# A retention, routed-experts and MLP kernel in which the conversion of the float64 weights, the experts' low parts and the second expert product are rewritten

## The chip, the cores and the metric

One core of a Trainium2 chip runs the whole program. The metric is the device time of one execution in microseconds (us), as the median of several runs. Times inside the execution come from one profiled execution of the kernel before.

Engines are named as the profile names them: PE is TensorE (PEld its weight loads), DVE is VectorE, ACT is ScalarE, POOL is GpSimd, SP is SyncE, which here only issues DMAs.

## What is computed

The reference has three parts, one behind the other, on 4608 tokens of 512 features:

```python
# retention: 8 batches x 8 heads, 576 positions, 64 features a head
scores = (1 / sqrt(64)) * q @ k.T
Dmat = where(rel >= 0, gamma[h] ** rel, 0)             # rel = i - j
x = (scores * Dmat) @ v                                # -> [4608, 512]

# routed experts: the tokens with a positive skip score, each to one of 8
do_compute = x @ w_skip > 0
xc = x[do_compute]
logits = xc @ w_gate
e_idx = argmax(logits, axis=1); gate = softmax(logits)[e_idx]
y = gate * (maximum(xc @ w1[e_idx], 0) @ w2[e_idx])    # w1 512x1024, w2 1024x512
x[do_compute] = xc + y

# MLP: w_in 512x2048 and w_out 2048x512 are float64
h = x @ w_in
out = (h * clip(h + 3, 0, 6) / 6) @ w_out
```

All inputs but `w_in` and `w_out` are float32. Those two arrive as float64 bits, and the kernel makes float32 pairs of them itself.

## The kernel before

**Numbers as pairs.** Products of float32 numbers are taken in the matmul type float32r. A factor is split into a high part (the number rounded to float32r) and a low part (the number less its high part), and a product is three matmuls: high by high, low by high, high by low. So every weight and every activation needs a copy (the high part, mostly on ScalarE) and a subtraction (the low part, on VectorE or GpSimd).

**Stages.** `phase_a` is the retention and the routing: a loop over 35 token tiles of 128 (`scale`, `scores`, `state`, `decay`, `rows`, the gate's products, and, four tiles at a time, the routing), then the last tile's routing, and eight blocks of the MLP's first product for 256 early tokens. `phase_b` is the experts, with more of the early blocks beside and behind the last one. `phase_c` is the MLP: 9 groups of 512 tokens by 16 blocks of inner features.

**Experts.** An expert takes 336 tokens, three tiles of 112 (`CT`). Its weights are 8 chunks of 128x1024 float32. The loop is over 8 experts `e` and 8 steps `f`, one step for 128 of the 1024 inner features. In a step, `mm1(e, f)` is 12 matmuls of 336 columns (line 889) into `h`; ScalarE makes `hh` (line 892), VectorE `hl` (line 894). Two steps later `mm2` is 12 matmuls of 336 columns (line 905): the weights are the stationary operand, and the four results `y` hold features on partitions and tokens in columns. Behind the last step of an expert, `y_out` copies the four `y` to `ys` in SBUF (lines 914 and 916), and `finish` turns them back to token rows with four transposes a tile (line 923), scales by the gate and adds the old row (line 925, VectorE), and scatters the rows to the table `xd` with an indirect DMA on GpSimd's queue (line 927). `finish` of expert e-1 stands in steps 2, 3 and 4 of expert e. `gather(e + 2)` stands in step 6 (line 865, three indirect DMAs); the rows of expert e+1 are turned in steps 5, 6 and 7: four transposes, then ScalarE's high part (line 881) and VectorE's low part (line 882) of `x`.

**The experts' weights.** A chunk is loaded into one of three buffers `raw` by SP, its high part is made by ScalarE (`chunk_hi`, line 156), its low part by GpSimd (`chunk_lo`, line 159). `pump_load`, `pump_hi` and `pump_lo` run ahead of the use, the low part 6 chunks (`LEAD`), the load 9. All 64 chunks pass in this way, six of them during the tile loop.

**The float64 weights.** They are taken in pieces of 256 columns (`CW`): 16 in the tile loop (`PARTX`, for the early blocks), 36 in the experts (`PART1`, stored as pairs to `wsc` in DRAM and loaded again later), 12 in the MLP (`PART2`). For a piece, `conv1` is six VectorE instructions on the two 32-bit words of each number (lines 207 to 217): four that build float32 bits from the high word `b`, two that turn the low word into a correction `a`. `conv_hi` is ScalarE's high part of `b`. `conv2` is two VectorE instructions: `b` less its high part (line 237), and `a` added to that (line 238). Three pieces are in work at a time, one stage apart.

**What sets the order.** Each engine runs its instructions in the order of the program text (`manual_schedule`), so the place of a call in a loop is its place in the engine's queue. A pool's buffer is handed to the next user when all readers of the last one are through.

Of the kernel before, what the change touches and what calls it, by code (L numbers as in the profile page):

```python
# [8 lines left out]
F32 = mybir.dt.float32  # L9
# [24 lines left out]
CONV_F = (0, 1, 3, 5, 6, 7)  # L34
# [21 lines left out]
def retention_moe_mlp_kernel(  # L56
    ctx: ExitStack,
    tc: tile.TileContext,
    qkv: bass.AP,      # [NT, 128, 4, 512]: q^T, k^T, k, v of a tile
    wg: bass.AP,       # [512, 32]: 8 gate columns, the skip column, zeros  # L60
# [8 lines left out]
    w_in, w_out = w_in.bitcast(I32), w_out.bitcast(I32)     # float64, as pairs of words  # L69
# [4 lines left out]
    ide = small[:, 0:4].rearrange("p (t c) -> p t c", c=2)        # early tokens  # L74
    ido = small[:, 4:10].rearrange("p (t c) -> p t c", c=2)       # the others of their tiles
# [4 lines left out]
    chp = prep.enter_context(tc.tile_pool(name="chp", bufs=3, side="right"))  # L80
    xp = prep.enter_context(tc.tile_pool(name="xp", bufs=1, side="right"))
# [35 lines left out]
    # ---------------------------------------------------------------- weights  # L117
    # chunk: [128, 1024] of float32 as two float32r parts, high and low
# [16 lines left out]
    # a chunk's place: the expert's 16 in turn, then the first the places that come free first  # L135
# [22 lines left out]
    def chunk_lo(i):  # L158
        nc.gpsimd.tensor_tensor(out=w_t[i][:, 1, :], in0=raw_t.pop(i), in1=w_t[i][:, 0, :].bitcast(F32), op=ALU.subtract)  # L159
# [24 lines left out]
    AH = [((f // 8) * 4, f % 8 // 2) for f in A_F[::2]]      # chunk of the first features, piece: a column group of xw  # L184
    PX = [(c + k, h) for c, h in AH for k in range(KD)]
# [4 lines left out]
    xw = {}            # w_in for the blocks A_F by feature tile; what they make behind it  # L190

    def conv_load(j):
        c, h = PIECES[j]
        src = chunk_src(64 + c)
        if c >= 8:
            src, h = src[:, h // (CN // 2), :], h % (CN // 2)
        r = cvp.tile([P, CW, 2], I32, tag="raw64", name="raw64")
        nc.sync.dma_start(out=r.rearrange("p n c -> p (n c)"), in_=src[:, h * 2 * CW:(h + 1) * 2 * CW])
        raw64[j] = r

    def conv1(j):
# [1055 lines left out]
```

## Time and profile before

| | us |
|---|---|
| median of 3 runs | 1425.91 |
| lowest, highest | 1423.62, 1426.36 |
| span of the profiled execution | 1422.7 |
| TensorE busy in it | 1293.4 (91%) |
| VectorE busy | 695.7 (49%) |
| ScalarE busy | 401.7 (28%) |
| GpSimd busy | 518.3 (36%) |

For the profiled execution the profile gives the span, from the first instruction to the last, and no time beside it; the median of the runs is 3.2 us above that span.

How the views are read. A stretch of the profiled execution is given as start:end in us from its start. The view by stretch shows its length and then, for PE, PEld, DVE, ACT and POOL, the busy time with the number of instructions, and last the granted clock of TensorE (1.00 is full speed), the mean busy share of the 16 DMA engines, and GB/s. The view by line gives the line of the code, the engine, the operation, output<-inputs by their names in the program, the tile's shape and type, the number of instructions, busy us, the mean ns of one, and the idle time of the engine before them with what ended it. In the view of waits, "PE h L889 <- DVE x L882" means that TensorE's instructions at line 889 waited for VectorE's at line 882. Busy time includes what an instruction spends waiting once it has begun.

### The profile page before, as it was taken

How to read it: one execution, taken by the hardware profiler on the slowest of the kernel's cores; microseconds unless marked ns; L12 is line 12 of the kernel's file. 1: busy time of each engine (PE TensorE's matmuls, PEld its weight loads, DVE VectorE, ACT ScalarE, POOL GpSimd, SP SyncE). 2: the span in 40 equal slices, each digit the busy share in tenths (PEclk: the TensorE clock that was granted, in tenths of full speed). 3: DMA queues.
4: the chain of work that ended last, by engine and by line, in shares of the span. 5: the costliest groups of instructions: out<-in, count | busy, mean ns of one | idle time of the engine just before them, and what ended most of it. 6: DMA issues, size and time to landing. Idle time of an engine off the chain costs nothing.

```text
span 1422.7 us, 20460 instructions
## 1 busy us (share of the span) xinstructions
PE 1293.4 (91%) x7973; PEld 1103.3 (78%) x7973; DVE 695.7 (49%) x1277; ACT 401.7 (28%) x724; POOL 518.3 (36%) x396
## 2 busy tenths in 40 slices
PE   8886878987788678999999999999999999999995
PEld 6665656986788677988888888888888888888884
DVE  6999998699999998259111111111111111111110
ACT  2222222533333333233222222222222222222221
POOL 4556455745664555222223222223222222222221
PEclk9999899998898888999999999999999999999998
DMA  9989683646565665853101000001000010000000
GB/s 349 255 244 304 219 294 127 202 154 197 181 199 175 195 205 168 333 200 104 67 1 42 26 23 30 23 8 37 23 30 17 14 38 23 30 1 1 30 0 31
DMA packets 71492, 163.60 MB, mean 115 GB/s; under 512 B 10420, under 2 KB 26804, under 8 KB 65504
## 3 DMA queue, kind: packets, MB, share of 16 engines
q1 hardware_dynamic: 63840, 146.38, 31.2%
q0 software_dynamic: 6592, 15.01, 3.4%
q8 instruction: 64, 1.05, 0.3%
q10 hardware_dynamic: 960, 0.86, 0.2%
q14 instruction: 36, 0.29, 0.1%
HBM read 121.47 MB, written 41.52 MB: 115 GB/s over the span
## 4 chain that ended last, share of the span: by engine, by line
PE 69%; DVE 25%; issue 2%; DMA 2%; ACT 0%; POOL 0%; SPq 0%; ACTq 0%; DVEq 0%; POOLq 0%
PE o L1102 28%; PE ch L1077 26%; DVE cvb L237 6%; PE y L905 4%; PE h L889 4%; DVE cva L207 3%; DVE ret L407 2%; DVE cva L209 2%; PE eh L269 2%; DVE kp L387 1%; DVE st L441 1%; DVE cvb L213 1%; PE cpt L1066 1%; DVE hl L894 1%; PE xTp L463 1%
## 5 line engine op out<-in xcount | busy, mean ns | idle before, releaser
L1077 PE MATMUL ch<-cx,w 128*128 128x512 f32 (+1 forms) x1728 | 397.6, 379 | 0.0
L1088 POOL TENSOR_TENSOR gl<-gt,gh 128x512 fp32r<-128x512 f32 (+1 forms) x144 | 178.2, 1237 | 601.2 <-ACT gh L1087 597.7
L1081 DVE SCALAR_TENSOR_TENSOR gt<-r,ch 128x512 f32<-128x512 f32 (+1 forms) x144 | 94.7, 658 | 579.3 <-ACT r L1079 579.3
L1102 PE MATMUL o<-w,gh 128*128 128x512 f32 x1120 | 377.8, 398 | 0.0
L1077 PEld LDWEIGHTS ch<-cx,w 128*128 128x128 f32 x1728 | 313.3, 188 | 66.1
L1102 PEld LDWEIGHTS o<-w,gh 128*128 128x128 f32 x1120 | 210.7, 188 | 47.9
L1102 PE MATMUL o<-w,gl 128*128 128x512 f32 x560 | 221.5, 395 | 0.0
L1079 ACT ACTIVATE r<-ch,small 128x512 f32<-128x512 f32 (+1 forms) x144 | 95.5, 663 | 431.4 <-PE ch L1077 431.4
L889 PE MATMUL h<-x,w 128*128 128x336 f32 x768 | 139.3, 332 | 63.9 <-DVE x L882 39.5
L889 PEld LDWEIGHTS h<-x,w 128*128 128x128 f32 x768 | 127.6, 200 | 67.9 <-DVE x L882 41.7
L159 POOL TENSOR_TENSOR w<-raw,w 128x1024 fp32r<-128x1024 f32 x64 | 152.4, 2397 | 60.5 <-ACT w L156 60.1
L905 PE MATMUL y<-hh,w 128*128 128x336 f32 x512 | 138.3, 337 | 0.0
L1087 ACT CAST gh<-gt 128x512 fp32r<-128x512 f32 (+1 forms) x144 | 86.1, 598 | 137.3 <-DVE gt L1081 136.8
L1102 PEld LDWEIGHTS o<-w,gl 128*128 128x128 f32 x560 | 105.5, 188 | 22.9
L237 DVE TENSOR_TENSOR cvb<-cvb,cvh 128x256 f32<-128x256 f32 x36 | 100.3, 2786 | 0.0
L905 PEld LDWEIGHTS y<-hh,w 128*128 128x128 f32 x512 | 95.9, 201 | 0.0
L905 PE MATMUL y<-hl,w 128*128 128x336 f32 x256 | 84.3, 329 | 0.0
L156 ACT CAST w<-raw 128x1024 fp32r<-128x1024 f32 x64 | 67.1, 1050 | 55.3 <-DMA raw<-in_w_dram 54.2
L467 ACT COPY xT<-xTp 128x512 f32<-128x512 f32 x36 | 21.1, 585 | 157.4 <-PE xTp L463 157.4
L892 ACT ACTIVATE hh<-h 128x336 fp32r<-128x336 f32 x64 | 28.8, 450 | 107.7 <-PE h L889 107.4
L927 POOL DMA_INDIRECT xd<-xr,ent x24 | 23.0, 957 | 88.1 <-DVE xr L925 86.4
L429 POOL TENSOR_TENSOR old<-st,cst 128x512 f32<-128x512 f32 x24 | 35.1, 1463 | 50.5 <-DVE st L441 33.8
(177 smaller groups left out, 1387.4 us busy)
## 6 DMA issues: line engine op xcount, KB each, us to landing
in<-in_qkv_dram SPq DMA_DIRECT2D x33, 1024.0 KB, 7.2
raw<-in_w_dram SPq DMA_DIRECT2D x64, 512.0 KB, 4.9
w<-wsc SPq DMA_DIRECT2D x13, 1024.0 KB, 9.6
xd<-row SPq DMA_DIRECT2D x36, 256.0 KB, 8.1
wsc<-cvh SPq DMA_DIRECT2D x36, 256.0 KB, 4.1
raw<-in_w_in_dram SPq DMA_DIRECT2D x32, 256.0 KB, 6.5
raw<-in_w_out_dram SPq DMA_DIRECT2D x32, 256.0 KB, 2.8
cr<-xd SPq DMA_DIRECT2D x31, 256.0 KB, 2.7
```

What stands on the lines that cost most here:

```text
L156: nc.scalar.copy(out=w_tile(i)[:, 0, :], in_=raw_t[i])
L159: nc.gpsimd.tensor_tensor(out=w_t[i][:, 1, :], in0=raw_t.pop(i), in1=w_t[i][:, 0, :].bitcast(F32), op=ALU.subtract)
L207: nc.vector.tensor_scalar(out=a, in0=hi32, scalar1=0x07FFFFFF, scalar2=3, op0=ALU.bitwise_and, op1=ALU.logical_shift_left)
L237: nc.vector.tensor_tensor(out=b.bitcast(F32), in0=b.bitcast(F32), in1=hl[:, 0, :].bitcast(F32), op=ALU.subtract)
L889: nc.tensor.matmul(out=h, lhsT=w_t[8 * e + k][:, lw, f * P:(f + 1) * P], rhs=rx[:, k, :], start=n == 0, stop=n == 11)
L905: nc.tensor.matmul(out=y_t[e][d], lhsT=w[:, lw, d * P:(d + 1) * P], rhs=rh, start=f == 0 and n == 0, stop=f == 7 and n == 2)
L1077: nc.tensor.matmul(out=h, lhsT=w_block(f)(k)[:, lw, :], rhs=rx[:, k, :], start=i == 0, stop=i == 11)
L1079: nc.scalar.activation(out=r, in_=h, func=AF.Relu, scale=1.0 / 6.0, bias=bias_half)
L1081: nc.vector.scalar_tensor_tensor(out=gt, in0=r, scalar=1.0, in1=h, op0=ALU.min, op1=ALU.mult)
L1087: nc.scalar.copy(out=gh[:, 0:n], in_=gt)
L1088: nc.gpsimd.tensor_tensor(out=gl[:, 0:n], in0=gt, in1=gh[:, 0:n].bitcast(F32), op=ALU.subtract)
L1102: nc.tensor.matmul(out=o_t[g][t], lhsT=lg[:, sl], rhs=w[:, rw, :], start=f == 0 and n == 0, stop=f == NF - 1 and n == 2)
```

## The change

1. `CW` is 512: 8, 18 and 6 pieces for 16, 36 and 12.
2. The conversion of a piece is built anew. The value is rounded to float32 once: `b` is first the absolute value of the high word (ScalarE, `AF.Abs`), then `a` the float32 bits, zeroed where `b` is under `TINY`, then `b` the correction, then `b = a + b`. The high part is a copy of that sum, the low part one subtraction. VectorE does seven instructions for a piece in place of eight, in three calls of `conv_step` instead of one, and these stand in every step of experts 1 to 7, and in the tile loop from the fourth tile on in three tiles of four. Pieces of the early blocks are stored there too.
3. `chunk_lo` goes from GpSimd to VectorE.
4. `mm2` takes the activations as stationary operand: 9 matmuls of 512 columns (three tiles, three products) into three `y` with 112 tokens on partitions. `y_out`, `ys` and the transposes of `finish` go. `finish` reads `y` in PSUM directly; its three tiles follow the last `mm2` of their expert, which is in step 1 of the next one.
5. `gather(e + 1)` stands in step 2 of expert e (from e = 1), where `gather(e + 2)` stood in step 6; the rows have two buffers, before three.
6. Buffers: the pairs of pieces (`chp`) have two buffers of twice the size instead of three; the initial table `tinit` takes a buffer of the tile loop's `ret`; the scratch of `further` and the MLP's output rows take buffers of the conversion; early blocks 4 to 7 lie in two `chp` buffers. Three warming matmuls before the last `finish` go.

The diff, cut to its core (comments are taken out all through the file, and line numbers move by that):

```diff
-    CW = 256           # columns of a piece
+    CW = 512
...
-        nc.gpsimd.tensor_tensor(out=w_t[i][:, 1, :], in0=raw_t.pop(i), in1=w_t[i][:, 0, :].bitcast(F32), op=ALU.subtract)
+        nc.vector.tensor_tensor(out=w_t[i][:, 1, :], in0=raw_t.pop(i), in1=w_t[i][:, 0, :].bitcast(F32), op=ALU.subtract)
...
+    def conv_a(j):
...
+        nc.scalar.activation(out=b, in_=hi32.bitcast(F32), func=AF.Abs)
...
         nc.vector.tensor_scalar(out=a, in0=hi32, scalar1=0x07FFFFFF, scalar2=3,
                                 op0=ALU.bitwise_and, op1=ALU.logical_shift_left)
         nc.vector.scalar_tensor_tensor(out=a, in0=hi32, scalar=-0x40000000, in1=a,
                                        op0=ALU.bitwise_and, op1=ALU.bitwise_or)
...
+    def conv_b(j):
...
+        nc.vector.scalar_tensor_tensor(out=a.bitcast(F32), in0=b, scalar=TINY, in1=a.bitcast(F32),
                                        op0=ALU.is_ge, op1=ALU.mult)
...
+        nc.vector.tensor_single_scalar(out=b.bitcast(I32), in_=a, scalar=-0x800000, op=ALU.bitwise_and)
+        nc.vector.scalar_tensor_tensor(out=b, in0=lo32.bitcast(U32), scalar=2.0 ** -52, in1=b, op0=ALU.mult, op1=ALU.mult)
+        nc.vector.tensor_tensor(out=b, in0=a.bitcast(F32), in1=b, op=ALU.add)
...
-        nc.vector.tensor_tensor(out=b.bitcast(F32), in0=b.bitcast(F32), in1=hl[:, 0, :].bitcast(F32), op=ALU.subtract)
-        nc.vector.tensor_tensor(out=hl[:, 1, :], in0=b.bitcast(F32), in1=a.bitcast(F32), op=ALU.add)
+        nc.vector.tensor_tensor(out=hl[:, 1, :], in0=b, in1=hl[:, 0, :].bitcast(F32), op=ALU.subtract)
...
     def conv_step(part):
...
+        j, i = divmod(cj[0], 3)
+        j += part.start
+        if i == 0:
+            if j - 1 in part:
+                conv_lo(j - 1)
+            if j in part:
+                conv_a(j)
+        elif i == 1:
+            if j in part:
+                conv_b(j)
+            if j + 1 in part:
+                conv_load(j + 1)
+            if part is not PART2 and j - 1 in part:
+                conv_store(j - 1)
+        elif j in part:
+            conv_hi(j)
...
-                r = xp.tile([CT, 3, D], F32, tag="xr0", name="xr0") if e % 3 == 0 else b2.tile([CT, 3, D], F32, tag="xr", name="xr")
+                r = b2.tile([CT, 3, D], F32, tag="xr", name="xr")
...
-                    y_t[e] = [py.tile([P, CAP], F32, tag="y", name=f"y{d}") for d in range(KD)]
+                    y_t[e] = [py.tile([P, D], F32, tag="y", name=f"y{t}") for t in range(3)]
                 w = w_t[8 * e + 4 + f // 2][:, :, (f % 2) * 512:(f % 2 + 1) * 512]
-                for d in ds:
-                    for n, (lw, rh) in enumerate(((0, hh), (0, hl), (1, hh))):
-                        nc.tensor.matmul(out=y_t[e][d], lhsT=w[:, lw, d * P:(d + 1) * P], rhs=rh,
+                for t in ts:
+                    sl = slice(t * CT, (t + 1) * CT)
+                    for n, (lg, rw) in enumerate(((hh, 0), (hl, 0), (hh, 1))):
+                        nc.tensor.matmul(out=y_t[e][t][0:CT, :], lhsT=lg[:, sl], rhs=w[:, rw, :],
                                          start=f == 0 and n == 0, stop=f == 7 and n == 2)
...
-                p = pt.tile([P, D], F32, tag="pt", name="py")
-                for d in range(KD):
-                    nc.tensor.transpose(p[0:CT, d * P:(d + 1) * P], ys_t[e][:, d, t * CT:(t + 1) * CT], ident)
                 o = rows_t[e][:, t, :]
-                nc.vector.scalar_tensor_tensor(out=o, in0=p[0:CT, :], scalar=ent[:, e, t, 1:2].bitcast(F32), in1=o,
+                nc.vector.scalar_tensor_tensor(out=o, in0=y_t[e][t][0:CT, :], scalar=ent[:, e, t, 1:2].bitcast(F32), in1=o,
...
                 if f == 7:
-                    for d in range(KD):
-                        y_out(e, d)
+                    for t in range(3):
+                        finish(e, t)
...
-                    if f in (2, 3, 4):
-                        finish(e - 1, f - 2)
...
-                    if f == 6:
-                        gather(e + 2)
+                    if f == 2 and e > 0:
+                        gather(e + 1)
...
-                    if f in CONV_F and 8 * e + f > 5:
+                    if 8 * e + f > 7:
                         conv_step(PART1)
```

VectorE's queue in the experts, kernel before, over one and a half steps of a middle expert (a row is line, operation, output<-inputs, tile; `cva`, `cvb`, `cvh` are the conversion's buffers, `raw_4634` its float64 words, `py` the turned-back result):

```order
L894 SCALAR_TENSOR_TENSOR hl<-h,hh 128x336
L925 SCALAR_TENSOR_TENSOR xr<-py,ent,xr 112x512
L237 TENSOR_TENSOR cvb<-cvb,cvh 128x256
L238 TENSOR_TENSOR cvh<-cvb,cva 128x256
L207 TENSOR_SCALAR cva<-raw_4634 128x256
L209 SCALAR_TENSOR_TENSOR cva<-raw_4634,cva 128x256
L212 TENSOR_SCALAR cvb<-raw_4634 128x256
L213 SCALAR_TENSOR_TENSOR cvb<-cvb,cva 128x256
L216 TENSOR_SCALAR cva<-cvb 128x256
L217 SCALAR_TENSOR_TENSOR cva<-raw_4634,cva 128x256
L894 SCALAR_TENSOR_TENSOR hl<-h,hh 128x336
```

The same queue in the changed kernel, from step 1 of an expert on (`y_4630` to `y_4632` are the results in PSUM of the expert before, `w<-raw,w` is the low part of a chunk):

```order
L892 SCALAR_TENSOR_TENSOR hl<-h,hh 128x336
L909 SCALAR_TENSOR_TENSOR xr<-y_4630,ent,xr 112x512
L909 SCALAR_TENSOR_TENSOR xr<-y_4631,ent,xr 112x512
L909 SCALAR_TENSOR_TENSOR xr<-y_4632,ent,xr 112x512
L159 TENSOR_TENSOR w<-raw,w 128x1024
L239 TENSOR_TENSOR cvh<-cvb,cvh 128x512
L207 TENSOR_SCALAR cva<-raw_4862 128x512
L209 SCALAR_TENSOR_TENSOR cva<-raw_4862,cva 128x512
L892 SCALAR_TENSOR_TENSOR hl<-h,hh 128x336
L159 TENSOR_TENSOR w<-raw,w 128x1024
L217 SCALAR_TENSOR_TENSOR cva<-cvb,cva 128x512
L220 TENSOR_SCALAR cvb<-cva 128x512
```

The three additions of an expert now stand together in front of a low part, each step has a low part behind its `hl`, and a piece of 512 columns is spread over three steps.

GpSimd's queue in the experts, before, over one expert (`xd` is the table of rows in DRAM; a scatter writes it, a gather `xr` reads it):

```order
L927 DMA xd<-xr_4038,ent 4609x512
L159 TENSOR_TENSOR w<-raw,w 128x1024
L927 DMA xd<-xr_4038,ent 4609x512
L159 TENSOR_TENSOR w<-raw,w 128x1024
L927 DMA xd<-xr_4038,ent 4609x512
L159 TENSOR_TENSOR w<-raw,w 128x1024 x3
L865 DMA xr_5331<-xd,ent 112x512 x3
L159 TENSOR_TENSOR w<-raw,w 128x1024 x3
```

And in the changed kernel, over three experts:

```order
L911 DMA xd<-xr,ent 4609x512 x3
L863 DMA xr<-xd,ent 112x512 x3
L911 DMA xd<-xr,ent 4609x512 x3
L863 DMA xr<-xd,ent 112x512 x3
L911 DMA xd<-xr,ent 4609x512 x3
L863 DMA xr<-xd,ent 112x512 x3
```

The low parts are gone from it, and the gathers stand right behind the scatters of the expert before.

TensorE's queue, before, over one step in which a tile is turned back (`x_4388` and `x_4389` are the high and low parts of the turned rows):

```order
L889 MATMUL h<-x_4388,w 128x336 x8
L889 MATMUL h<-x_4389,w 128x336 x4
L923 MATMUL py<-ident,ys 112x128 x4
L905 MATMUL y_4680<-hh,w 128x336
L905 MATMUL y_4680<-hl,w 128x336
L905 MATMUL y_4680<-hh,w 128x336
L905 MATMUL y_4681<-hh,w 128x336
L905 MATMUL y_4681<-hl,w 128x336
L905 MATMUL y_4681<-hh,w 128x336
L905 MATMUL y_4682<-hh,w 128x336
L905 MATMUL y_4682<-hl,w 128x336
L905 MATMUL y_4682<-hh,w 128x336
```

(the three of `y_4683` follow). The same step in the changed kernel:

```order
L887 MATMUL h<-x_5085,w 128x336 x8
L887 MATMUL h<-x_5086,w 128x336 x4
L904 MATMUL y_5299<-w,hh 112x512
L904 MATMUL y_5299<-w,hl 112x512
L904 MATMUL y_5299<-w,hh 112x512
L904 MATMUL y_5300<-w,hh 112x512
L904 MATMUL y_5300<-w,hl 112x512
L904 MATMUL y_5300<-w,hh 112x512
L904 MATMUL y_5301<-w,hh 112x512
L904 MATMUL y_5301<-w,hl 112x512
L904 MATMUL y_5301<-w,hh 112x512
```

The transposes are gone, and nine matmuls of 512 columns stand where twelve of 336 stood.

## Rows read from the trace of the kernel before

**Rows 1.** Busy time of each engine by stretch: us, engines' busy, granted clock, DMA.
```profile
0.00:26.50 26.50, 23.58 (x268) 17.58 (x270) 15.04 (x27) 4.47 (x8) 13.11 (x27) 0.94 0.94 350
26.50:235.30 208.80, 163.05 (x2064) 130.91 (x2059) 197.30 (x431) 54.48 (x124) 115.14 (x90) 0.92 0.81 254
...
262.50:615.10 352.60, 288.91 (x1822) 282.90 (x1823) 298.20 (x452) 119.94 (x211) 188.72 (x114) 0.89 0.62 204
615.10:1422.70 807.60, 792.31 (x3593) 649.54 (x3591) 167.19 (x293) 210.62 (x353) 186.23 (x152) 0.99 0.10 32
```

**Rows 2.** Waits of TensorE in the experts: total us, times, longest us.
```profile
PE h L889 <- DVE x L882: 39.5, 6, 7.5
PE h L889 <- ACT x L881: 17.6, 6, 3.9
```

**Rows 3.** Timeline in the experts: start us, duration us, engine, line, operation.
```profile
412.49 7.76 DVE L237 TENSOR_TENSOR cvb<-cvb,cvh 128x256 f32<-128x256 f32 x1
412.87 7.10 POOL L159 TENSOR_TENSOR w<-raw,w 128x1024 fp32r<-128x1024 f32 x3
...
420.13 1.02 POOL L865 DMA_INDIRECT xr<-xd,ent  x1 [0.16 <-issue]
420.29 0.43 DVE L238 TENSOR_TENSOR cvh<-cvb,cva 128x256 fp32r<-128x256 f32 x1
...
421.62 0.29 DVE L212 TENSOR_SCALAR cvb<-raw 128x256 int32<-128x256 int32 x1
```

**Rows 4.** VectorE in the experts by line: busy us, mean ns, idle before.
```profile
L237 DVE TENSOR_TENSOR cvb<-cvb,cvh 128x256 f32<-128x256 f32 x36 | 100.3, 2786 | 0.0
L894 DVE SCALAR_TENSOR_TENSOR hl<-h,hh 128x336 fp32r<-128x336 f32 x64 | 32.1, 502 | 30.7 <-ACT hh L892 30.6
...
L925 DVE SCALAR_TENSOR_TENSOR xr<-py,ent,xr 112x512 f32<-112x512 f32 x24 | 17.8, 743 | 1.5 <-PE py L923 1.5
...
L882 DVE TENSOR_TENSOR x<-pt,x 128x448 fp32r<-128x448 f32 x22 | 13.5, 614 | 0.4 <-ACT x L881 0.4
```

**Rows 5.** Whole execution by line and shape, two lines.
```profile
L159 POOL TENSOR_TENSOR w<-raw,w 128x1024 fp32r<-128x1024 f32 x64 | 152.4, 2397 | 60.5 <-ACT w L156 60.1
...
L407 DVE TENSOR_TENSOR ret<-s,cst 128x1024 f32<-128x1024 f32 x35 | 42.6, 1218 | 0.8
```

**Rows 6.** The chain that ended last, 255 to 640: start us, us, what.
```profile
488.74 0.44 PE py L923 x4
...
569.76 1.85 PE h L889 x12
...
589.47 1.42 PE eh L269 x12
...
613.81 1.31 PE bw L96 x6
...
628.55 1.40 PE o L1102 x6
```

**Rows 7.** DMA issues: KB each, median us from issue to landing.
```profile
raw<-in_w_dram SPq DMA_DIRECT2D x64, 512.0 KB, 4.9
...
xr<-xd,ent POOLq DMA_INDIRECT x24, 3.6
xd<-xr,ent POOLq DMA_INDIRECT x24, 5.2
```

**Rows 8.** VectorE in the tile loop by line.
```profile
L387 DVE TENSOR_TENSOR kp<-in,cst 128x512 f32<-128x512 f32 x27 | 18.7, 692 | 0.8
L237 DVE TENSOR_TENSOR cvb<-cvb,xw 128x256 f32<-128x256 f32 x16 | 17.1, 1067 | 0.0
...
L216 DVE TENSOR_SCALAR cva<-cvb 128x256 int32<-128x256 int32 x16 | 4.7, 294 | 0.5
```

**Rows 9.** GpSimd in the tile loop by line.
```profile
L381 POOL TENSOR_TENSOR qp<-in,cst 128x512 f32<-128x512 f32 x28 | 35.8, 1279 | 9.9 <-PE xTp L455 5.2 <-issue 4.1
L429 POOL TENSOR_TENSOR old<-st,cst 128x512 f32<-128x512 f32 x21 | 30.6, 1457 | 48.3 <-DVE st L441 31.6 <-DVE st L439 16.7
```

More of the change, by code (lines that the diff above doesn't have):

```diff
@@ L32 @@
 OVT = N // P + E + 2
-CONV_F = (0, 1, 3, 5, 6, 7)
 NW = 13
@@ L181, in retention_moe_mlp_kernel @@
     raw64, tmp_t, hl_t = {}, {}, {}
-    CW = 256
+    CW = 512
     CN = 1024 // CW
-    AH = [((f // 8) * 4, f % 8 // 2) for f in A_F[::2]]
-    PX = [(c + k, h) for c, h in AH for k in range(KD)]
+    PX = [(4 + k, h) for h in range(CN) for k in range(KD)]
     P1 = [(c, h) for c in range(NW) for h in range(CN) if (c, h) not in PX]
@@ L194, in conv_load @@
         src = chunk_src(64 + c)
-        if c >= 8:
-            src, h = src[:, h // (CN // 2), :], h % (CN // 2)
+        src = src[:, h, :] if c >= 8 else src[:, h * 2 * CW:(h + 1) * 2 * CW]
         r = cvp.tile([P, CW, 2], I32, tag="raw64", name="raw64")
-        nc.sync.dma_start(out=r.rearrange("p n c -> p (n c)"), in_=src[:, h * 2 * CW:(h + 1) * 2 * CW])
+        nc.sync.dma_start(out=r.rearrange("p n c -> p (n c)"), in_=src)
         raw64[j] = r
-    def conv1(j):
-        raw = raw64.pop(j)
-        lo32, hi32 = raw[:, :, 0], raw[:, :, 1]
+    def conv_a(j):
+        raw = raw64[j]
+        hi32 = raw[:, :, 1]
         a = cvp.tile([P, CW], I32, tag="cva", name="cva")
-        b = cvp.tile([P, CW], I32, tag="cvb", name="cvb")
+        b = cvp.tile([P, CW], F32, tag="cvb", name="cvb")
+        nc.scalar.activation(out=b, in_=hi32.bitcast(F32), func=AF.Abs)
         nc.vector.tensor_scalar(out=a, in0=hi32, scalar1=0x07FFFFFF, scalar2=3,
@@ L271, in rest @@
         def rest():
-            r = cvp.tile([P, CW], I32, tag="cva", name="ge").bitcast(F32)
+            r = cvp.tile([P, CW], I32, tag="cva", name="ge").bitcast(F32)[:, 0:PN]
             nc.scalar.activation(out=r, in_=h, func=AF.Relu, scale=1.0 / 6.0, bias=bias_half)
@@ L627, in clear @@
                 n = E * ER // P
-                tinit = a1.tile([P, 2 * n], I32, name="tinit")
+                tinit = ap.tile([P, 2 * n], I32, tag="ret", name="tinit")
                 tv = tinit.rearrange("p (s c) -> p s c", c=2)
@@ L680, in early_block @@
                     g6.append(place(6, (P, 4, 2, PN), "ge"))
+                if i == 4:
+                    g8.extend(chp.tile([P, 2, 2, PN], F32R, tag="cvh", name="cvh") for _ in range(2))
                 early(f, h, lambda k: xw[k][:, :, n:n + P],
-                      g6[0][:, i] if i < 4 else chp.tile([P, 2, CW], F32R, tag="cvh", name="cvh") if i < 7 else xw[0][:, :, 0:CW])
+                      g6[0][:, i] if i < 4 else g8[i // 2 - 2][:, i % 2])
             for k in range(KD):
                 xw[k] = place(8 + k, name="xw")
+            cj[0] = 0
             todo, ranks = [], []
             L = NT - 1
-            C1 = [t for t in range(3, 33) if t % 4 in (3, 0)]
-            C2 = [t + 1 if t % 4 == 3 else min(t + 2, L - 2) for t in C1]
             scale(0)
@@ L709, in phase_a @@
                 if t == L - 1:
+                    conv_step(PARTX)
+                    conv_step(PARTX)
                     break
@@ L742, in phase_a @@
                 gate_mm(t - 1)
-                if t in C2:
-                    conv2(C2.index(t))
-                if t in C1:
-                    conv1(C1.index(t))
+                if t > 2 and t % 4 != 2:
+                    conv_step(PARTX)
                 if t % 3 == 1 and t > 15:
@@ L807, in further @@
             def further():
-                mem = b1.tile([P, KD, CAP], F32, tag="ys", name="o_mem").rearrange("p k c -> p (k c)")
+                mem = cvp.tile([P, CW, 2], I32, tag="raw64", name="o_mem").rearrange("p n c -> p (n c)").bitcast(F32)
                 used = [0]
@@ L936, in phase_b @@
                 early_store(f, nc.gpsimd)
-            cj[0] = PART1.start
+            cj[0] = 0
             conv_load(PART1.start)
@@ L997, in phase_b @@
             out_step()
-            for d in range(KD):
-                mm2(*lag[0], ds=[d])
-                y_out(E - 1, d)
-            warm(ph.tile([P, 512], F32, tag="h", name="bw"), 3)
-            finish(E - 1, 0)
-            finish(E - 1, 1)
+            for t in range(3):
+                mm2(*lag[0], ts=[t])
+                finish(E - 1, t)
             rest = early_late(G_F[0], keep[1][:, 1], later=True)
-            finish(E - 1, 2)
             rest()
@@ L1104, in mm2 @@
                     if f == NF - 1 and g < NG:
-                        o = c3.tile([P, D], F32, tag="co", name="cos", bufs=4)
+                        o = cvp.tile([P, D], F32, tag=("cva", "raw64")[t // 2], name="cos")
                         if t % 2:
@@ L1113, in phase_c @@
             pump_load(80)
-            cj[0] = PART2.start
-            conv_move(PART2)
-            conv_step(PART2)
+            cj[0] = 0
             for f in range(EF):
@@ L1125, in phase_c @@
                     lag.append((g, f, *mm1(g, f)))
-                    if g == 0 and (f > 4 or f % 2 == 0) and cj[0] < PART2.stop + 2:
-                        conv_move(PART2)
-                        conv_step(PART2)
+                    if g == 0:
+                        for _ in range(2 - f % 2):
+                            conv_step(PART2)
                     if f in (6, 8, 10, 12):
@@ L1178, in phase_c @@
                     mm2(NG, f, *mm1(NG, f), (0,))
-                o = c3.tile([P, D], F32, tag="co", name="cox", bufs=4)
+                o = cvp.tile([P, D], F32, tag="cva", name="cox")
                 nc.vector.tensor_copy(out=o, in_=o_t[NG][0])
```

59 lines of the change are left out of this document (13 added, 46 removed).

## Prediction, made before the changed kernel was run

> **What bounds the kernel now.** I read the busy time by stage first [rows 1]. The span of 1422.7 us falls into five stretches: a start, the tile loop of the retention (26.5 to 235.3), the last routing with the early blocks, the experts (262.5 to 615.1), and the MLP. In the MLP TensorE is busy 792.3 of 807.6 us at a granted clock of 0.99, and the change takes no TensorE work out of it. In the tile loop VectorE is busy 197.3 of 208.8 us and TensorE 163.1. In the experts VectorE has 298.2 of 352.6 us, TensorE 288.9 at a clock of 0.89. So VectorE sets the pace in the first two and TensorE in the last.
>
> Then the waits of TensorE in the experts [rows 2]: 39.5 us for VectorE's part of the turned rows `x`, in six waits, one per expert boundary, and 17.6 us for ScalarE's part of the same rows. VectorE is late, so the next question is what holds it. By line [rows 4], 36 subtractions of 256 columns (L237) take 100.3 us, 2786 ns each. The timeline shows why [rows 3]: L237 starts at 412.49 and ends at 420.25, just behind three GpSimd low parts (L159) that run from 412.87 to 419.97; the next one of the same shape takes 0.43. A VectorE instruction with two SBUF operands lasts until GpSimd's tensor instruction is out of the way. 36 undisturbed ones would be 15.5 us, so 85 us of VectorE's stage are this wait.
>
> The Trainium skill, "SBUF — State Buffer" (Who interferes with whom), says that such an instruction and a GpSimd instruction that reads SBUF shut each other out for a whole instruction, and that who starts first decides. These rows agree: one L237 outlasts three L159.
>
> **The change, part by part.**
>
> *Low parts on VectorE.* 64 subtractions of 128x1024 leave GpSimd, 2397 ns each [rows 5]. VectorE has not run this shape from SBUF; the ends are 1.22 (L407, the same columns, one operand from PSUM) and 2.40 (GpSimd's). I take 1.22, the same engine and width. Six fall in the tile loop (7.3 us), 58 in the experts (70.8 us). What GpSimd keeps in the experts up to the early blocks is indirect DMAs, 48 of them; beside one of these a two-operand VectorE instruction took 0.43 [rows 3], so they block nothing that I can see. The 85 us go.
>
> *Conversion.* A piece is 512 columns instead of 256: 18 pieces in the experts for 36, 8 in the tile loop for 16, 6 in the MLP for 12. VectorE does seven instructions instead of eight, five with two operands and two `tensor_scalar`. A two-operand 128x512 is 0.69 (L387, [rows 8]). The `tensor_scalar` is 0.29 at 256 columns [rows 3], so 0.29 to 0.69 at 512; I take 0.45, nearer its own row. A piece: 5 x 0.69 + 2 x 0.45 = 4.35. ScalarE gets one more pass of some 0.6 per piece; it was busy 119.9 of 352.6 [rows 1], and loses 16 copies.
>
> *Second product.* Per step, 12 matmuls of 336 columns become 9 of 512. Rows [rows 6]: 12 of 336 take 1.85; 6 of 512 in the MLP take 1.40, hence 9 take 2.10. That is +0.25 x 64 = +16.0. The 24 groups of four transposes back to token rows go, 0.44 each, -10.6, and three warming matmuls, -0.7 (six take 1.31). TensorE's work grows by some 5 us: taken alone this part is a loss. What it saves elsewhere is the PSUM copies (16 on VectorE).
>
> *Experts, sum.* TensorE: 64 x (1.85 + 2.10) = 252.8; turning rows, 21 x 0.44 = 9.2; early blocks, 8 x 1.42 = 11.4; warming 1.3; together 274.7. VectorE in a middle expert: 8 hl x 0.50 + 3 x x 0.61 + 3 finish x 0.74 [rows 4] + 8 low parts x 1.22 + 8/3 pieces x 4.35 = 29.4 against TensorE's 8 x 3.95 + 1.3 = 32.9. VectorE falls below TensorE, at 89% of it. I add 4 for waits at the start and beside the last expert, where 1 MB weight loads now meet conversion stores. 278.7, against 352.6: -74. Bounds: nothing lost, -78; VectorE still pacing, -49 (below).
>
> *New waits in the experts.* The gather of an expert's rows moves from step 6 two experts ahead to step 2 of the expert before, right behind three scatters on GpSimd's queue, into the buffer that these read. The last finish ends some 4.9 after step 1 begins (1.85 + 2.10 + 0.74 and a little); a descriptor run is 1.0 [rows 3], a scatter lands in 5.2, a gather in 3.6 [rows 7]: the first rows are there about 15 after step 1 begins. TensorE turns them behind the first product of step 5, 4 x 3.95 + 1.85 = 17.7. So it is hidden by 2 to 3 us for the first tile and more for the others; what is missing there, each expert would lose. The finish waits on VectorE for the second product, up to 2 us, with a low part and a piece behind it; `hl` is needed two steps later, so this is hidden too.
>
> *Tile loop.* The eight conversion lines are 80.2 us there (first L237, 17.1; last L216, 4.7; [rows 8]). Undisturbed, 16 pieces cost 16 x (3 x 0.29 + 5 x 0.42) = 47.5, so 32.7 is waiting, 2.0 per piece, for GpSimd's `qp`, `old` and low parts. The first two, 35.8 and 30.6 us, stay [rows 9]. After: 8 x 4.35 = 34.8, waiting 8 x 2.0 = 16.4, six low parts 7.3: 58.5. Saved 21.7 (ends: 0, if all 40 two-operand and 16 other instructions wait as L237 does here, 0.65 each, and the low parts too; 38 with no waiting). By the skill's rule above the six low parts wait as well, up to 1.46 each (`old`): 8.8 more. The table's blank rows now sit in one of the two buffers of `ret`, so two of the first tiles share the other and wait for the product in front: up to 3 us, which I subtract. -18. TensorE's 163 leaves room.
>
> *MLP.* TensorE is full there; 6 pieces x 4.35 = 26 on VectorE's idle time, before 12 pieces. Output rows move to the conversion's buffers, four as before. 0, within 3 either way.
>
> Sum: 1422.7 - 18 - 74 = 1331 for the profiled execution. The median shown, 1425.91, lies 3.2 above its span, so 1334.
>
> **The rivals.**
>
> VectorE stays the bound in the experts (0.15). For it: low parts, which GpSimd did aside, now stand in the queue in front of `hl`, and each waits for ScalarE's high part and its load; 89% leaves little. Against: the slack of two steps. If the waits add 3.1 us per expert, 36 instead of 32.9, it is +25: 1359. The Trainium skill, "Perfetto Trace Analysis" (Optimizing Scalar/DVE Operations), warns that moving work between these two engines may not help, since they share a port. Rows 5 speak against it here: the work takes half the time on VectorE.
>
> The tile loop doesn't shrink (0.10): four fifths of GpSimd's tensor work stays there (66.4 us, beside six low parts of 2.4, [rows 5, 9]), and the DMA share is 0.81 already [rows 1]. +18: 1352.
>
> Better than forecast (0.06): the tile loop follows VectorE's relief and TensorE's wait there too, -35, no loss in the experts: 1313.
>
> Slower than before (0.03): the load chain. Three raw buffers: a load waits for the low part three chunks back, and VectorE waits, in order, for the high part of that load. A round may take three steps, 12.3 us. The bytes of the stage, 204 GB/s x 352.6, have to pass in 279 us: 258 GB/s at a share of 0.78; 350 was reached in the first stretch [rows 1]. Landing is 4.9 in the median [rows 7]. It would have to reach about 12 for this to decide; at 13 a step is 5.8, the experts 64 x 5.8 + 22 = 393, the whole 1448.
>
> **How the numbers follow.** Forecast 0.66, with its own range 1320 to 1348. Range to be given: 1308 (better case with its spread) to 1368 (VectorE bound, with a little of the tile loop's failing); it leaves out the slower case and the far ends. Within 0.2% of 1425.9, about what a measurement of this kernel can't tell from no change, is only a point between cases: 0.01. Faster 0.96, slower 0.03.
>
> **What would show it.** Right: no VectorE instruction of the experts above 1.4 us; TensorE's stage some 279 long at a clock near 1.0, its waits for `x` gone; 8 steps some 33 us apart; L237's excess gone; the tile loop near 190. Wrong: TensorE waiting for `hl` or `x` behind low parts (first rival), for `xr` (the gather), ScalarE for raw loads (fourth), or VectorE in the tile loop still above 190 busy.

## The result, and the profile after

The changed kernel takes 1368.93 us (median of 4 runs, 1366.72 to 1371.35); the kernel before, beside it, 1424.76. The ratio is 0.961, with a 95% interval of 0.959 to 0.963. It is 56 us faster, where 92 were forecast: the direction was right, and the time lies 0.9 us above the range given.

By stretch, cut at the same places of the program as [rows 1] (length, busy us of PE, PEld, DVE, ACT and POOL, granted clock, DMA share, GB/s):

```profile
0.00:26.50 26.50, 22.33 (x273) 16.44 (x274) 14.38 (x25) 4.59 (x9) 13.76 (x27) 1.00 0.94 362
26.50:223.20 196.70, 159.79 (x2056) 127.49 (x2054) 176.18 (x363) 57.48 (x124) 102.65 (x84) 0.93 0.84 267
...
251.30:553.30 302.00, 281.68 (x1529) 245.30 (x1530) 207.56 (x332) 121.25 (x194) 64.04 (x56) 0.97 0.70 237
553.30:1365.00 811.70, 793.64 (x3594) 649.24 (x3592) 156.75 (x240) 213.78 (x353) 186.30 (x152) 0.99 0.09 32
```

| stretch | before | after | difference | forecast |
|---|---|---|---|---|
| tile loop | 208.8 | 196.7 | -12.1 | -18 |
| last routing, early blocks | 27.2 | 28.1 | +0.9 | 0 |
| experts | 352.6 | 302.0 | -50.6 | -74 |
| MLP | 807.6 | 811.7 | +4.1 | 0 |
| span | 1422.7 | 1365.0 | -57.7 | -92 |

So 23.3 of the missing 34 us are in the experts. VectorE is not what holds them now: it is busy 207.6 of 302.0 us. Its lines there, as in [rows 4]:

```profile
L159 DVE TENSOR_TENSOR w<-raw,w 128x1024 fp32r<-128x1024 f32 x58 | 70.3, 1214 | 0.0
L892 DVE SCALAR_TENSOR_TENSOR hl<-h,hh 128x336 fp32r<-128x336 f32 x64 | 32.3, 505 | 54.8 <-ACT hh L890 54.7
...
L909 DVE SCALAR_TENSOR_TENSOR xr<-y,ent,xr 112x512 f32<-112x512 f32 x24 | 16.5, 741 | 1.8 <-PE y L904 1.8
...
L239 DVE TENSOR_TENSOR cvh<-cvb,cvh 128x512 fp32r<-128x512 f32 x18 | 12.3, 685 | 0.0
```

The low part costs 1214 ns (taken: 1.22), and the subtraction of the conversion, 2786 ns for 256 columns in [rows 4], is 685 ns for 512 (taken: 0.69). The wait of 85 us is gone, as forecast. What TensorE waits for now is another thing; its largest wait in the experts, as in [rows 2] (total us, times, longest):

```profile
PE pt L877 <- DMA xr<-xd,ent: 20.3, 6, 4.6
```

Line 877 turns the gathered rows of the next expert. The timeline of one boundary (start us, duration us, engine, line; in brackets the idle time before, and what ended it):

```profile
324.25 2.06 DVE L909 SCALAR_TENSOR_TENSOR xr<-y,ent,xr 112x512 f32<-112x512 f32 x3
...
325.27 0.98 POOL L911 DMA_INDIRECT xd<-xr,ent  x1 [20.25 <-DVE xr L909]
326.22 1.22 DVE L159 TENSOR_TENSOR w<-raw,w 128x1024 fp32r<-128x1024 f32 x1
326.56 2.66 POOL L911 DMA_INDIRECT xd<-xr,ent  x1 [0.30 <-DVE xr L909]
...
329.52 1.95 POOL L911 DMA_INDIRECT xd<-xr,ent  x1 [0.30 <-DVE hl L892]
...
337.78 1.01 POOL L863 DMA_INDIRECT xr<-xd,ent  x1 [6.31 <-DMA xd<-xr,ent]
...
343.53 0.98 PE L877 MATMUL pt<-ident,xr 112*128 112x112 f32 x4 [4.56 <-DMA xr<-xd,ent]
```

The three scatters (L911) are issued one behind the other, the second taking 2.66 us and the third 1.95 where the first takes 0.98. No gather (L863) is issued before the third scatter has landed, since the three tiles of an expert's rows lie in one buffer, and the gather writes into it. The landings (as [rows 7], median us) are later than before too, 5.8 for 5.2 and 5.6 for 3.6:

```profile
xr<-xd,ent POOLq DMA_INDIRECT x24, 5.6
xd<-xr,ent POOLq DMA_INDIRECT x24, 5.8
```

The wait costs more than its length. In the 4 us behind it (343.5 to 347.5) the granted clock is at half, which is 1.2 of 2.4 GHz. So it is behind four of the six waits, those of 3.0 to 4.6 us; behind the other two, of 2.2 and 2.8, it stayed at full speed.

```profile
330.00:343.50 13.50, 8.97 (x50) 7.69 (x48) 8.44 (x13) 4.53 (x7) 4.46 (x4) 0.96 0.89 283
343.50:347.50 4.00, 3.97 (x12) 3.14 (x13) 2.36 (x3) 1.48 (x2) 0.00 (x0) 0.50 0.01 4
```

### The profile page after: what moved, and what is told of

It is laid out like the page before. It is cut to its first block, busy times and chain, and to the rows that moved or that the text cites. A ratio compares the mean times of both kernels' runs of the same rounds, so it can differ in the third digit from the quotient of the medians.

```text
span 1365.0 us, 19313 instructions
## 1 busy us (share of the span) xinstructions
PE 1283.1 (94%) x7682; PEld 1061.0 (78%) x7682; DVE 573.8 (42%) x1037; ACT 409.4 (30%) x708; POOL 381.2 (28%) x332
## 3 DMA queue, kind: packets, MB, share of 16 engines
q8 instruction: 62, 1.02, 0.3%
## 4 chain that ended last, share of the span: by engine, by line
PE 69%; DVE 10%; issue 10%; DMA 7%; POOL 2%; ACT 1%; POOLq 0%; ACTq 0%; SPq 0%; DVEq 0%
PE o L1078 29%; PE ch L1053 27%; PE y L904 4%; DMA xd<-xr,ent 3%; PE h L887 3%; PE eh L272 2%; DVE ret L410 2%; DMA xd<-row 1%; DMA xr<-xd,ent 1%; PE cpt L1042 1%; PE xTp L466 1%; DVE st L444 1%; DVE kp L390 1%; POOL xd L911 1%; PE xTp L458 1%
## 5 line engine op out<-in xcount | busy, mean ns | idle before, releaser
L904 PE MATMUL y<-w,hh 128*112 128x512 f32 x384 | 136.7, 411 | 0.0
L887 PE MATMUL h<-x,w 128*128 128x336 f32 x768 | 129.3, 318 | 0.6 <-ACT x L879 0.6
L887 PEld LDWEIGHTS h<-x,w 128*128 128x128 f32 x768 | 123.7, 190 | 7.0 <-ACT x L879 0.8
L904 PEld LDWEIGHTS y<-w,hh 128*112 128x112 f32 x384 | 69.8, 182 | 19.5
L911 POOL DMA_INDIRECT xd<-xr,ent x24 | 36.3, 1512 | 171.7 <-DVE xr L909 169.3
L159 DVE TENSOR_TENSOR w<-raw,w 128x1024 fp32r<-128x1024 f32 x64 | 78.8, 1234 | 0.0
L904 PE MATMUL y<-w,hl 128*112 128x512 f32 x192 | 77.7, 405 | 0.0
L156 ACT CAST w<-raw 128x1024 fp32r<-128x1024 f32 x64 | 67.0, 1049 | 12.4 <-DMA raw<-in_w_dram 11.7
L470 ACT COPY xT<-xTp 128x512 f32<-128x512 f32 x36 | 21.1, 586 | 150.6 <-PE xTp L466 150.6
L892 DVE SCALAR_TENSOR_TENSOR hl<-h,hh 128x336 fp32r<-128x336 f32 x64 | 32.3, 505 | 54.8 <-ACT hh L890 54.7
```

Of the source, the lines that this page charges most:

```text
L156: nc.scalar.copy(out=w_tile(i)[:, 0, :], in_=raw_t[i])
L159: nc.vector.tensor_tensor(out=w_t[i][:, 1, :], in0=raw_t.pop(i), in1=w_t[i][:, 0, :].bitcast(F32), op=ALU.subtract)
L887: nc.tensor.matmul(out=h, lhsT=w_t[8 * e + k][:, lw, f * P:(f + 1) * P], rhs=rx[:, k, :], start=n == 0, stop=n == 11)
L904: nc.tensor.matmul(out=y_t[e][t][0:CT, :], lhsT=lg[:, sl], rhs=w[:, rw, :], start=f == 0 and n == 0, stop=f == 7 and n == 2)
L911: own_rows("xd", nc.gpsimd.indirect_dma_start(out=xd, out_offset=bass.IndirectOffsetOnAxis(ent[:, e, t, 0:1], 0), in_=o, in_offset=None, b ...
```

## The experiments

Theory: the gathers, held until the third scatter has landed, are what the experts lost. Rivals: the transfers are late whatever their order; VectorE is still too full. Each kernel is compared by its ratio to runs of the kernel before on the same chip, since one and the same kernel differs by some 10 us from chip to chip (the kernel before: 1424.76 to 1434.24).

**Rows in three buffers of one tile (split).**

```diff
-                r = b2.tile([CT, 3, D], F32, tag="xr", name="xr")
+                r = [b2.tile([CT, D], F32, tag=f"xr{t}", name="xr") for t in range(3)]
...
```

> The changed kernel, its gathered rows in three buffers of one tile each instead of one buffer of three tiles, so that the gather of a tile waits for the scatter of that tile alone. Theory G (the gather's wait): in the changed kernel all three gathers wait until the third scatter has landed, some 12 us behind the first scatter, and TensorE then waits 20.3 us in six boundaries, at a lower clock behind each. Here the first gather can go out right behind the third scatter's issue, some 6 us sooner: TensorE's waits for gathered rows fall from 20.3 to under 5 us, the experts from 302 to 280-285 us, the whole by 17 to 22 us. Rival D (traffic): the rows land late because the DMA engines are fuller than before (share 0.70 for 0.62) and GpSimd writes descriptors slowly; then over 12 us of the waits stay and the whole moves by less than 8 us.

Measured: 0.938 (0.936 to 0.939), 33 us under the changed kernel's ratio. The experts, 257.8 to 534.4, and TensorE's wait there:

```profile
257.80:534.40 276.60, 273.02 (x1530) 239.08 (x1531) 207.60 (x333) 121.42 (x194) 66.25 (x53) 1.00 0.77 258
```

```profile
PE pt L877 <- DMA xr<-xd,ent: 3.6, 4, 1.2
```

The experts take 276.6 us, the waits are 3.6, and the clock is 1.00. DMA is fuller than in the changed kernel (0.77 for 0.70), and the scatters are issued as slowly (1514 ns on the mean, 1512 there), so with the order alone changed the waits go: rival D falls. VectorE is as busy as before (207.6 us), so it was not too full either. The gain is larger than expected. Of it 25.4 us are in the experts, 16.7 by shorter waits and 8.7 by TensorE's busy time (281.7 to 273.0); the rest lies between two chips and was not taken apart.

**The changed kernel, low parts back on GpSimd (after_lo_gpsimd).** The edit is one word, `nc.vector` to `nc.gpsimd` in `chunk_lo`.

> The changed kernel with the low parts back on GpSimd, all else as changed. Theory P (VectorE's two-operand instructions wait for GpSimd's tensor instructions): the low parts stop them again and stand behind scatters and gathers that wait on GpSimd's queue; single VectorE instructions of 2 us and more come back, the experts get 20 to 50 us longer. Rival (it was the rewritten conversion, with fewer instructions): VectorE has room now, 58 x 1.22 = 71 us less to do, and the experts stay within 5 us of 302.

Measured: 0.974 (0.972 to 0.976), about 18 us above the changed kernel's ratio; the experts take 316.9 us (on another chip than the 302.0). The seven conversion lines at 512 columns in the experts:

```profile
L239 DVE TENSOR_TENSOR cvh<-cvb,cvh 128x512 fp32r<-128x512 f32 x18 | 32.0, 1779 | 0.0
L209 DVE SCALAR_TENSOR_TENSOR cva<-raw,cva 128x512 int32<-128x512 int32 x18 | 31.9, 1774 | 0.6
L221 DVE SCALAR_TENSOR_TENSOR cvb<-raw,cvb 128x512 f32<-128x512 uint32 x18 | 28.5, 1582 | 0.6
L217 DVE SCALAR_TENSOR_TENSOR cva<-cvb,cva 128x512 f32<-128x512 f32 x18 | 25.2, 1398 | 0.0
L207 DVE TENSOR_SCALAR cva<-raw 128x512 int32<-128x512 int32 x18 | 22.3, 1236 | 9.4 <-DMA raw<-in_w_in_dram 5.1 <-DMA raw<-in_w_out_dram 4.3
...
L220 DVE TENSOR_SCALAR cvb<-cva 128x512 int32<-128x512 int32 x18 | 16.1, 894 | 0.6
...
L222 DVE TENSOR_TENSOR cvb<-cva,cvb 128x512 f32<-128x512 f32 x18 | 12.5, 692 | 0.6
```

Theory P holds: the waiting comes back, spread over six of the seven lines (each 0.43 to 0.70 with the low parts gone). Two of the six, L207 and L220, are `tensor_scalar` with one operand, so not only two-operand instructions are stopped. The price is under the 20 to 50 expected. A likely part of the reason is that the scatters' issues were quick here (1091 ns on the mean) and TensorE waited only 10.1 us for gathered rows.

**The kernel before with the low parts on VectorE (before_lo_vector).** The same word the other way, and nothing else.

> The kernel before with the low parts on VectorE and nothing else changed. Theory P: the waiting of the 36 subtractions (85 us) goes, 58 x 1.22 = 71 us of low parts come, and since the work is spread evenly over the steps VectorE comes to about 32 us an expert, even with TensorE: experts from 352 to 280-305, the whole 45 to 75 us faster, which is most of what the full change gave. Rival (moving work between the two engines doesn't help, since VectorE gets nearly as much work as it loses in waiting): within 15 us of the kernel before.

Measured: 0.953 (0.951 to 0.954), 68 us faster, and better than the whole change. The experts, and the line that had 2786 ns in [rows 4]:

```profile
270.30:558.80 288.50, 273.16 (x1820) 266.90 (x1821) 240.37 (x509) 120.90 (x210) 59.92 (x46) 0.99 0.74 242
```

```profile
L237 DVE TENSOR_TENSOR cvb<-cvb,cvh 128x256 f32<-128x256 f32 x36 | 15.1, 419 | 0.0
```

This one word carries the gain in the experts. The gather stands two experts ahead there, with three buffers, and no wait for gathered rows shows at the boundary; TensorE's largest waits in the experts are 8.5 us for `x` and 6.2 for the copies `ys`.

**The kernel before with only the second product changed (before_mm2_tokens).** `mm2`, `finish` and the calls of `finish` as in the change; gathers, conversion and low parts as before.

> The kernel before with the second product's tokens on partitions, its three additions behind the last step of the expert, no turning back; low parts, conversion and gathers as before. Theory: taken alone it does not pay: TensorE gets 16 us more matmuls and loses 11 us of transposes, VectorE, which paces the experts, loses 16 copies of some 0.5 us: between -10 and +8 us. Rival (the turning back was part of the boundary's wait): over 15 us faster.

Measured: 1.007 (1.006 to 1.009), 10 us slower, just outside the range expected, and on the loss side. TensorE's waits in the experts, and the VectorE line that now stands behind GpSimd's low parts:

```profile
PE h L889 <- DVE hl L894: 41.5, 6, 9.2
PE h L889 <- DVE x L882: 23.7, 6, 4.4
```

```profile
L213 DVE SCALAR_TENSOR_TENSOR cvb<-cvb,cva 128x256 f32<-128x256 int32 x36 | 67.1, 1865 | 1.2
```

The collision only moved, from L237 (450 ns now) to L213 and L238 (1179 ns): with another order of VectorE's queue other instructions meet the low part.

**The changed kernel again (after_again).**

> The changed kernel once more, so that the others of this group stand beside it on the same chip. Expected: the ratio of the first time, 0.961 (0.959 to 0.963), and TensorE's waits for gathered rows near 20 us in six boundaries.

Measured: 0.959 (0.956 to 0.962), waits for gathered rows 24.3 us.

**Low part and piece out of steps 1 and 2 (quiet_step).**

```diff
-                    pump_lo(8 * e + f + LEAD - (e + f == 1))
+                    pump_lo(8 * e + (0 if f in (1, 2) and e > 0 else f) + LEAD - (e + f == 1))
...
-                    if 8 * e + f > 7:
-                        conv_step(PART1)
+                    if 8 * e + f > 7 and f not in (1, 2):
+                        for _ in range(2 if f in (3, 4) else 1):
+                            conv_step(PART1)
```

> The changed kernel, with VectorE's low part and conversion piece left out of steps 1 and 2 of each expert and made up for in steps 3 and 4, so that little runs on VectorE beside the three scatters. The second scatter's issue takes 1.7 to 3.4 us on GpSimd in the changed kernel, the first, beside the addition, 1.0. Theory V (VectorE's two-operand instructions hold up GpSimd's descriptor writing): all three issues fall to 1.0-1.3 us, the last scatter goes out 2 us sooner, and TensorE's waits for gathered rows fall from 20 to 6-12 us, the whole by 8 to 15 us. Rival (descriptors take what they take, the landing decides): waits within 4 us of 20.

Measured: 0.957 (0.956 to 0.959), which can't be told from the changed kernel. Yet the boundary is another one. The same boundary, and TensorE's waits in the experts:

```profile
323.95 2.06 DVE L909 SCALAR_TENSOR_TENSOR xr<-y,ent,xr 112x512 f32<-112x512 f32 x3
...
324.97 0.98 POOL L911 DMA_INDIRECT xd<-xr,ent  x1 [24.58 <-DVE xr L909]
326.26 0.96 POOL L911 DMA_INDIRECT xd<-xr,ent  x1 [0.30 <-DVE xr L909]
...
327.53 0.94 POOL L911 DMA_INDIRECT xd<-xr,ent  x1 [0.30 <-issue]
...
331.36 1.01 POOL L863 DMA_INDIRECT xr<-xd,ent  x1 [2.89 <-PE h L887]
```

```profile
PE h L887 <- DVE hl L892: 10.9, 7, 3.8
PE h L887 <- DVE x L880: 4.6, 2, 2.6
PE h L887 <- ACT x L879: 2.5, 3, 1.6
PE pt L877 <- DMA xr<-xd,ent: 1.5, 2, 1.1
```

All three issues take about 0.95, as theory V has it, and the wait for rows falls from 24.3 to 1.5, more than expected. Shorter issues are the smaller part of that. From the end of the last addition to the third issue the path is 1.65 us on the mean of the six boundaries, for 2.98 in the changed kernel; from the third issue to the first gather it is 3.92, for 7.47. While the third scatter lands, the DMA engines are much less busy (the changed kernel first, then this one, from the third issue to the first gather of the boundary shown):

```profile
329.52:337.78 8.26, 8.26 (x47) 7.25 (x46) 7.26 (x12) 3.65 (x6) 1.95 (x2) 1.00 0.90 284
```

```profile
327.53:331.36 3.83, 3.83 (x23) 3.34 (x22) 0.48 (x2) 1.30 (x2) 0.94 (x1) 1.00 0.34 105
```

A low part frees the buffer `raw` of a later load, so moving it probably moves the weights' loads too; this edit then changes two things at once, and the rival, that the landing decides, has its share. And the work made up for in steps 3 and 4 stands in front of `hl` and `x` and costs 18.0 us of new waits: one wait traded for another. The next two runs take the two halves of the edit apart.

**Only the low part out of steps 1 and 2 (quiet_low_part), only the piece (quiet_piece).** Each has one of the two edits above.

> The changed kernel with only the low part left out of steps 1 and 2 of each expert (made up for in step 3); the pieces stay where they were. If the low part of 1.22 us is what holds up the second scatter's issue, issues fall to 1.0-1.7 us (a two-operand 128x512 of 0.69 may still stand in the way), their mean from 1512 to about 1100 ns, and TensorE's waits for gathered rows from 20-24 to 5-15 us; the three low parts in a row in step 3 cost 3 to 8 us of waits for hl. Whole between the changed kernel's ratio and 1% under it. If it is the conversion's instructions, issues stay near 1.5 us on the mean.

> The changed kernel with only the conversion piece left out of steps 1 and 2 of each expert (made up for in steps 3 and 4); the low parts stay. If the low part holds up the second scatter's issue, that stays at about 1.7 us (the rest of a low part of 1.22 and then 0.95), as where no piece follows in the changed kernel, the mean falls from 1512 to about 1250 ns only, and the waits for gathered rows to 10-18 us. If it is the piece, issues fall to 1.0.

Measured: low part out, 0.942 (0.939 to 0.946), waits for rows 3.2, for `hl` 1.6, experts 281.2 us, mean issue 1129 ns. Piece out, 0.953 (0.950 to 0.956), waits for rows 12.1, mean issue 1390 ns, the second scatter's issue 1.71 to 1.72 in the six boundaries behind the first (2.83). So the low part behind the additions is what mostly holds up the issues, and the piece adds to it. But with the low part out the landing is shorter too: from the third issue to the first gather 4.10 us on the mean, at a DMA share of 0.30 to 0.48, while with the piece out it is 6.67, at 0.77 to 0.86. Most of what the low part gave back is that, and not the issue. Its gain on the whole time is also more than the 1% expected, with shorter waits for `hl` than the 3 to 8 us. Both kernels stand apart from the changed kernel's 0.959 and 0.961, and the low part's interval lies clear below the piece's.

**No conversion on VectorE in the tile loop (no_tile_conversion).** `conv_a`, `conv_b` and `conv_lo` are replaced there by ScalarE's two passes alone.

> The changed kernel without VectorE's seven conversion instructions a piece in the tile loop (the early blocks' weights are then wrong); loads, ScalarE's two passes and stores stay. In the changed kernel VectorE lost 21 us of busy time in the tile loop and the loop only 12. Theory C (the chain between VectorE and TensorE from tile to tile is what is left): of the 52 us of VectorE's work that go here the loop gives back less than 20. Rival (VectorE still paces it): it gives back over 35 us.

Measured, in one run of each kernel: the loop beside that of the changed kernel on the same chip (no conversion first, then the changed kernel):

```profile
26.50:198.70 172.20, 154.98 (x2052) 123.89 (x2052) 132.71 (x307) 57.11 (x124) 100.14 (x83) 0.95 0.92 301
```

```profile
26.50:220.70 194.20, 160.87 (x2055) 128.86 (x2055) 176.26 (x362) 57.31 (x124) 102.87 (x84) 0.93 0.84 271
```

VectorE loses 43.6 us (52 was an overestimate), and the loop 22.0, half of it. That lies between the two expectations, nearer to theory C (under 20) than to its rival (over 35): VectorE idles 39.5 us of the shorter loop.

**Split rows, and the MLP's pieces spread (split_mlp).**

```diff
-                        for _ in range(2 - f % 2):
+                        for _ in range(1 if f < 6 else 2 - f % 2):
```

> The changed kernel with the gathered rows in three buffers of one tile each, and with one sub-step of a piece instead of two in every second of the first six steps of the MLP. In the changed kernel TensorE waits 1.3, 1.1 and 0.6 us there for VectorE's gt, behind two sub-steps (4.1 us), and the MLP is 3.8 us longer than before. Expected: these waits go, MLP 808 for 811.7, whole 2 to 4 us under the kernel with the split rows alone. Rival (the weights' loads from wsc, 13.4 us to landing for 9.6, hold it): the MLP stays at 811.

Measured: 0.937 (0.935 to 0.938), median 1334.37, the best of all. The experts (246.0 to 521.5) and the MLP behind them:

```profile
246.00:521.50 275.50, 272.73 (x1528) 238.98 (x1529) 206.98 (x332) 121.48 (x194) 68.88 (x56) 1.00 0.77 260
```

```profile
521.50:1329.40 807.90, 792.94 (x3595) 649.58 (x3593) 157.19 (x240) 214.61 (x353) 186.52 (x152) 0.99 0.10 32
```

The MLP is back at 807.9 (before: 807.6), so the waits for `gt` behind two sub-steps were its loss. On the whole time the 3 us don't stand out from the split rows alone: the intervals overlap.

## Why the prediction was wrong

**What held.** The stretch that matters (experts), its cause (VectorE's instructions stopped by GpSimd's low parts) and the prices: 1214 ns for 1.22, 685 for 0.69, `tensor_scalar` 446 for 0.45. VectorE's busy time in the tile loop came to 176.2, by the sum 197.3 - 21.7 = 175.6. TensorE's work in the experts, 274.7 by the sum, is 272.7 where nothing stops it, and the experts take 275.5 and 276.6 there, for 278.7 forecast. The judgement that the second product alone is a loss was right (+10 us).

**The step that failed.** "... the first rows are there about 15 after step 1 begins. TensorE turns them behind the first product of step 5 ... So it is hidden by 2 to 3 us ..." This path was too short, and so the wait for the gathered rows, put at nothing, was 20.3 us. In the boundary shown step 1 begins at 321.2, and TensorE is ready for the rows at 339.0, 17.7 later, as the prediction had it. The rows came at 343.5, 22.3 after. Of the terms of the 15, the additions' end held (5.1 for 4.9), and the rest was too small (5.1 + 1.6 + 1.6 + 7.4 + 0.9 + 5.7 = 22.3):
- The path runs over the third scatter, not the first. The issues alone, 1.3 us apart, put it 1.6 behind the end of the last addition (326.3).
- The issue of a scatter was held up by the low part and the piece behind it: the third began at 329.5, another 1.6 late. The prediction had read of the indirect DMAs that "they block nothing that I can see" on VectorE, and not asked the reverse.
- The scatter's landing: 7.4 us from the third issue's start, for 5.2; then 0.9 until the first gather begins.
- The gather: 5.7 from issue to TensorE's start, for 3.6.

The two landings are 4.3 of the 7.3 us that the sum was short. They came at DMA shares of 0.90 and 0.87 in this boundary; the medians taken were those of a kernel with 0.62 in the experts. That the order alone is enough to take the wait away is shown by the split rows, where the landings did not have to be shorter for it (in split_mlp the third scatters landed 6.2 to 7.2 us after their issue began).

It also priced a miss at its own length only. Of the 23.3 us, 20.3 are the wait itself, and TensorE's busy time, 272.7 where nothing stops it, is 281.7 here, 9.0 us more, at half the clock behind four of the six waits; the 4 us allowed for and 2 us of overestimated work go against that (272.7 + 20.3 + 9.0 = 302.0).

The Trainium skill, "SBUF — State Buffer" (Who interferes with whom), which the prediction drew on, says there too that a stalled DMA beside a VectorE instruction is one whose descriptors GpSimd writes, and infers that `tensor_tensor` does not cause it, since it takes only the read side of the shared ports. The first half agrees with the trace as far as it goes: it is issues on GpSimd's queue that last longer. The second does not: a `tensor_tensor` with both operands in SBUF (L159, 1.22 us) takes the second issue from 0.96 (without low part and piece) to 1.72 (without the piece), and the measurement decides. These DMAs are indirect ones and also take their row numbers from SBUF; which part of an issue is held was not taken apart.

Of the rule that the prediction cites from there, that who starts first decides, its "These rows agree" says too much. In [rows 3] L237 starts at 412.49, before the first low part (412.87), and is held all the same; in five more of the 36 cases it is so. In all six a scatter's issue was in work on GpSimd when L237 began, and whether that held it first was not taken apart.

**The tile loop.** VectorE's saving was taken as the loop's, and the loop gave back 12.1 of 21.1. VectorE waits there for TensorE now (idle 20.5 us, before 11.5), in a chain that goes to and fro from tile to tile. That the conversion's VectorE time is worth half its length there is shown by the run without it; why the other half stays was not taken apart, and the 6 us missed are not far above what the loop differs by from run to run (208.9 to 214.2 from its first to its last product `stp`, the `state` stage, in seven runs of the same loop). The shortest of them, in the run split_mlp, is 191.3 us by the stretch of the table, 17.5 under the kernel before. The six low parts there waited little: 8.6 us, for 7.3 without waiting and up to 8.8 more by the price that the prediction's rule gave.

**The MLP.** "0, within 3 either way" missed a size: two sub-steps of 512 columns, some 4.1 us, stand in front of `gt` (what VectorE makes of a block's first product) in steps of about 2.9 us, and TensorE waited 3.0 us for it, in three waits.

**The rivals.** The first had the nearest time (1359), but not the cause: VectorE was not the bound, 207.6 of 302.0. The load chain did not show: ScalarE waited 11.7 us in all for the experts' raw loads, in waits of at most 3.7. With the rows split and the pieces spread the kernel takes 1334.37 us, 91.5 under the kernel before on its chip, which is the 92 forecast for the change.

## What to carry to other kernels

A buffer that several transfers share is released by the last of them: where a gather follows scatters, one buffer a tile took the wait away here without any work being moved. Follow a hidden chain over its last member, with every issue in its queue and with landings as they are at the traffic to come, and ask of each engine pair in both directions who holds up whom. When one change has several parts, the part that removes the bound (here one word) should be timed alone: it beat the whole. And when an experiment moves work, see what else moves with it: here the DMA share behind the scatters fell from 0.90 to 0.34.

## What the runs showed of the hardware

- GpSimd's issue of a scatter took 0.94 to 1.02 us by itself or beside an addition, and longer where VectorE ran low parts: in the changed kernel 1.72 behind one low part, 2.32 behind a low part and a two-operand 128x512 instruction, 2.66 with a `tensor_scalar` behind these, 3.43 behind two low parts and a two-operand 128x512. These second issues ended some 0.85 after the last of the instructions named. Third issues (1.49 and 1.95) ended 0.8 after the low part, though a two-operand instruction followed it without a gap, so no one rule covers all.
- Gathers are held up too: 0.98 to 1.52 in the changed kernel, up to 2.01 in quiet_step, where two low parts ran beside one.
- A scatter landed 2.9 to 3.7 us after the start of its issue at a DMA share of 0.32 to 0.62 (third scatters of quiet_step), and 6.1 and 6.7 at 0.78 and 1.01 (two of the changed kernel whose landing shows).
- A wait of TensorE of 4.6 us was followed by 4 us at half its clock (0.50), with matmuls of 512 columns at 0.63 us for 0.40.
